# Three more attention units by rows, their projections spread, and the loads of the next group moved to other slots

## The chip, the cores and the metric

The kernel runs on one core of one Trainium2 chip. The metric is the device time of one launch in microseconds (us), the median of several runs. A profile is one of those executions; its "span" is some 2 us shorter than the device time. A run is called fast when it lies within 1.5% of the fastest run of the same kernel; only fast runs are compared.

## The reference, cut to what matters

One block with adaptive layer norms: grouped-query attention over a cache, then a gated MLP with a spatial projection.

```python
h = _layernorm(x, axis=-1) * (1 + ca) + sa          # sa, ca, ga, sb, cb, gb = split(silu(c) @ w_mod)
q = (h @ wq) ...                                     # 2048 rows, 32 heads of 128
scores = einsum('bhqd,bhkd->bhqk', q, k) * Dh ** -0.5  # 8 groups of K and V, 4 heads each, 2048 keys
o = einsum('bhqk,bhkd->bhqd', softmax(scores), v)
x = x + ga * (o @ wo)
... # second norm and the MLP, gated by gb
```

## The kernel before

The work is cut into 128 **units**: 8 groups of 4 heads times 16 tiles of 128 query rows. A unit has 8 **slots**; a slot is two QK matmuls of 512 columns (they make the scores) and one exponential on 128x1024. PV is the product of these exponentials with V. A unit is done in one of two ways. By columns, the scores come out transposed, PV needs 64 matmuls of 129 columns, and a small transpose by DMA (oT) follows. By rows, the scores come out with queries on partitions, each head is normalised on VectorE and turned by a DMA transpose of 128x2048 (pT; a **turn** below), and PV needs 16 matmuls of 512 columns, two units later than by columns. Even units from `TURN_A` on go by rows. The normalised and not yet turned rows of a head sit in `pn`, four buffers, each used again two units later.

```python
TURN_A, TURN_B = 3 * CT, (HKV - 1) * NT              # 12 and 112; CT = 4, NT = 16

def by_rows(u):
    return TURN_A <= u < TURN_B and u % 2 == 0

def pv_at(u):
    return u + 3 if by_rows(u) else u + 1            # so unit TURN_A + 1 has no PV: the "hole"

def turn_rows(u, hh):                                # two slots after a head's last exponential
    ...
    nc.vector.tensor_scalar(out=pn[hh], in0=pn[hh], scalar1=rinv, scalar2=None, op0=ALU.mult)
    nc.sync.dma_start_transpose(out=pTs[u][:, :, hh * P : (hh + 1) * P], in_=pn[hh])
```

`at(unit, slot, fn)` puts work at a place of the program. This is an order of issue per engine and no time: GpSimd, which has little to do, reaches a load long before TensorE reaches the slot, unless something stops it.

```python
ln1_at(1, (0, 7), (1, 2), (2, 2))     # chunk 1 of 4: statistics, norm (+ 4 DMA transposes), modulation
ln1_at(2, (2, 4), (3, 1), (4, 5))
ln1_at(3, (5, 1), (5, 5), (7, 4))
at(2, 5, lambda: nc.gpsimd.dma_start(out=wmod_b, in_=wmod_dram[:, :, 2 * D : NMOD]))   # 2 MB
at(9, 4, mod_cols_b)
at(10, 4, mod_rows)

def mod_rows():                       # the two gate rows, ga and gb
    ...                               # 32 matmuls of one column, result on partitions
    for i, (part, rows) in enumerate(((2, ga_rows), (5, gb_rows))):
        ...
        line = dram.tile([D], FP32, name=f"mod{part}")
        nc.gpsimd.dma_start(out=line[:].rearrange("(dt p) -> p dt", p=P), in_=modc[:, cols])
        nc.gpsimd.dma_start(out=rows[:], in_=line[:].partition_broadcast(P))
```

The last two lines, twice, are **the chain of the gate rows**: 2 KB written to memory as 512 pieces of 4 bytes, and read back to all partitions (256 KB).

Of the kernel before, what the change touches and what calls it, by code (L numbers as in the profile page):

```python
# [575 lines left out]
def kernel(  # L576
# [19 lines left out]
    nc = tc.nc  # L596
    _, S, D = A_x.shape
    _, HKV, SK, DH = A_k_cache.shape
# [4 lines left out]
    NMOD = w_mod.shape[1]  # L603
    assert DH == P and D == 512 and S % 512 == 0 and SK % 1024 == 0 and FH % P == 0 and REP == 4
    NT = S // P
# [4 lines left out]
    CT = 512 // P  # L610
    FC = _f_chunk(FH)
    NFHC = FH // FC
    NSLOT = NKT // 2
# [12 lines left out]
    wmod_dram = w_mod.rearrange("(p dt) n -> p dt n", p=P)  # L626
# [35 lines left out]
    wmod_b = wspp.tile([P, NDT * 4 * D], BF16, name="wsp")[:].rearrange(  # L662
        "p (k n) -> p k n", k=NDT
    )
# [53 lines left out]
    def load_wq(g, engine):  # L718
        wqs[g] = early.tile([P, NDT, REP * DH], BF16, name="wq_g")
        engine.dma_start(  # L720
            out=wqs[g][:], in_=wq_dram[:, :, g * REP * DH : (g + 1) * REP * DH]
        )

    def load_v(g):
        v1 = late.tile([P, NKT, DV], BF16, name="v1")
        nc.gpsimd.memset(v1[:, :, DH:DV], 1.0)
        if g > 0:
            nc.gpsimd.dma_start(out=v1[:, :, 0:DH], in_=v_dram[:, g])
        else:
            nc.sync.dma_start(out=v1[:, 0 : NKT // 2, 0:DH], in_=v_rows)  # L730
            nc.sync.dma_start(
                out=v1[:, NKT // 2 : NKT, 0:DH], in_=v_dram[:, 0, NKT // 2 : NKT]
            )
        groups[g]["v1"] = v1

    def load_wo(g, engine):
        wo_g = late.tile([P, REP, D], BF16, name="wo_g")
        engine.dma_start(out=wo_g[:], in_=wo_dram[:, g * REP : (g + 1) * REP, :])
        groups[g]["wo"] = wo_g

    def load_k(g):
        kT = early.tile([P, SK], BF16, name="kT")
        nc.sync.dma_start_transpose(out=kT[:], in_=A_k_cache[0, g])
        groups[g] = dict(kT=kT)
# [154 lines left out]
    for k in range(2):  # L899
        for dt in (2 * k, 2 * k + 1):  # L900
# [3 lines left out]
            else:  # L904
                nc.scalar.activation(
                    out=dst,
                    in_=src,
# [17 lines left out]
    for hf, copy in enumerate((nc.vector.tensor_copy, nc.scalar.copy)):  # L925
        copy(
            out=qTs[0][:, 2 * hf : 2 * hf + 2, 0:P],
            in_=q_ps[hf][:, 0 : 2 * P].rearrange("p (h q) -> p h q", h=2),
# [3 lines left out]
    def qproj(b, heads, c0, n, banks=("misc", "misc")):  # L932

        g, ch = divmod(b, NCH)
        if b not in qTs:
            qTs[b] = early.tile([P, REP, 512], BF16, name="qT")
        one = n * len(heads) <= 512
        ps = {}

        def mm(hh, dt):  # L940
            if dt == 0 and (not one or hh == heads[0]):
                ps[0] = bank(banks[hh % 2])
            o0 = (hh - heads[0]) * n if one else 0
            nc.tensor.matmul(  # L944
                ps[0][:, o0 : o0 + n],
                lhsT=wqs[g][:, dt, hh * DH : (hh + 1) * DH],
                rhs=hTs[ch][:, dt, c0 : c0 + n],
                start=(dt == 0),
                stop=(dt == NDT - 1),
            )  # L950
            if dt == NDT - 1 and (not one or hh == heads[-1]):
                hs = heads if one else [hh]
                dst = qTs[b][:, hs[0] : hs[-1] + 1, c0 : c0 + n]
                src = ps[0][:, 0 : len(hs) * n].rearrange("p (h q) -> p h q", q=n)
                nc.vector.tensor_copy(out=dst, in_=src)  # L955

        return [lambda hh=hh, dt=dt: mm(hh, dt) for hh in heads for dt in range(NDT)]
# [4 lines left out]
    NU = HKV * NT  # L962


    TURN_A, TURN_B = 3 * CT, (HKV - 1) * NT

    def by_rows(u):
        return TURN_A <= u < TURN_B and u % 2 == 0
# [7 lines left out]
    def at(it, slot, fn):  # L976
        later.setdefault((it, slot), []).append(fn)
# [230 lines left out]
    def ln1_at(ch, stats, norm, turn):  # L1208
        st = {}
        at(*stats, lambda: st.update(r=ln1_stats(ch * CT, CT)))  # L1210
        at(*norm, lambda: st.update(x=ln1_norm(ch * CT, CT, st["r"])))
        at(norm[0], norm[1] + 1, lambda: ln1_dma(ch * CT, CT, st["x"]))
        at(*turn, lambda: ln1_dma_mod(ch))
# [1 line left out]
    ln1_at(1, (0, 7), (1, 2), (2, 2))  # L1215
    ln1_at(2, (2, 4), (3, 1), (4, 5))
    ln1_at(3, (5, 1), (5, 5), (7, 4))
    at(2, 5, lambda: nc.gpsimd.dma_start(out=wmod_b, in_=wmod_dram[:, :, 2 * D : NMOD]))
    at(TURN_B + 3, 5, lambda: nc.gpsimd.dma_start(out=win_sb, in_=win_dram))
    at(9, 4, mod_cols_b)  # L1220
    at(10, 4, mod_rows)

    def set_fill(b):


        hole = TURN_A + 1 if (TURN_A + 1) // CT == b - 1 else None
        fs = qproj(b, list(range(REP)), 0, 512, ("misc", "o_ps" if hole else "misc"))
        for k, fn in enumerate(fs):
            it, slot = (b - 1) * CT + k // NDT, k % NDT
            if hole:  # L1230
                it, slot = hole, k // 2
            if b == 1:
                it, slot = 2 + (10 + k) // 16, (5 + k // 2) % 8
            elif b == 2:
                it, slot = (5, k // 2) if k < 8 else (it, slot)
            fill.setdefault((it, slot), []).append(fn)

    def wsp0():
# [4 lines left out]
        at(TURN_B + 4 + st // 2, 2 + 4 * (st % 2), lambda st=st: load_wsp(wsp[0], 0, st))  # L1243
    for g in range(1, HKV):
        it = (g - 1) * NT
        at(it + 7, 6, lambda g=g: load_k(g))
        at(it + 8, 3, lambda g=g: load_v(g))
        at(it + 9, 3, lambda g=g: load_wo(g, nc.gpsimd))
        at(it + 7, 3, lambda g=g: load_wq(g, nc.gpsimd))


    zs = {}
# [90 lines left out]
    for it in range(NU + 6):  # L1343
        if it < NU:
            if it % CT == 0 and it // CT + 1 < NB:
                set_fill(it // CT + 1)
        elif it == NU:
            free_a.close()
            z2p = fast.enter_context(tc.tile_pool(name="z2p", bufs=1))
            zs["z2"] = z2p.tile([P, NT, FH], BF16, name="z2")  # L1350
# [41 lines left out]
    for f in range(NFT):  # L1392
# [6 lines left out]
        out=ok1[:], in0=rall[:], scalar1=1.0 / SAFE, scalar2=None, op0=ALU.is_ge  # L1399
# [8 lines left out]
        out=bad[:], in0=okm[:], scalar1=-1.0, scalar2=1.0, op0=ALU.mult, op1=ALU.add  # L1408
# [137 lines left out]
```

## Time and profile before

| | before |
|---|---|
| device time, median of 4 runs | 1317.82 us (1315.36 to 1318.52) |
| span of the profiled run | 1314.1 us, granted clock 0.999 (share of TensorE's full clock) |
| pair of units by rows and by columns, steady state | 17.44 us |
| units 0 to 15, from the first exponential of 0 to that of 16 | 138.5 us |

The duration of a unit is read from the timeline of ScalarE: it is the distance between the first exponentials of two units. All unit durations below come from this view. The first fence is GpSimd's timeline (start, duration, instruction, idle time before it and what ended it), the second the timeline of the queue that issues the transposes.

```profile
113.98 0.56 POOL L1174 DMA_DIRECT2D ga_rows<-mod  x1 [8.27 <-DMA mod<-modc]
114.53 0.76 POOL L1173 DMA_DIRECT2D mod<-modc  x1
126.35 0.55 POOL L1174 DMA_DIRECT2D gb_rows<-mod  x1 [11.05 <-DMA mod<-modc]
```

```profile
121.41 12.66 SPq L1038 DMA_TRANSPOSE pT<-win_sb  x3
```

The chain runs from 104.96 us (the first write) to 126.35. The first turn of all is issued at 121.41, so the writes and the turns share only the last 5 us.

### The profile page before, as it was taken

The page shows a single profiled execution, that of the slowest core. Times are in us where ns is not written, and L with a number is a line of the kernel's source. Part 1 is how long each engine was busy: PE and PEld are TensorE (multiplying, and loading weights), DVE is VectorE, ACT ScalarE, POOL GpSimd, SP SyncE. Part 2 cuts the span into 40 slices and gives each one's busy share as a digit, 9 for nine tenths or more (in the row PEclk, how much of TensorE's full clock was granted, in tenths as well). Part 3 has the DMA queues.
Part 4 walks back from the last instruction along what each step waited for, and adds up shares of the span by engine and source line. Part 5 has one row for each costly group of instructions (what it writes and reads, how often), then busy time and mean ns, then how long its engine had stood idle before and what let it go on. Part 6 is the DMA issues. An engine that isn't in the chain of part 4 may idle for free.

```text
span 1314.1 us, 25092 instructions
## 1 busy us (share of the span) xinstructions
PE 1305.1 (99%) x9959; PEld 755.5 (57%) x9959; DVE 657.4 (50%) x1612; ACT 1105.0 (84%) x1461; POOL 52.0 (4%) x96
## 2 busy tenths in 40 slices
PE   9999999999999999999999999999999999999998
PEld 5666555555555555555555555555556666644445
DVE  6624445444454544444455544444452566784444
ACT  7899999999999999999999999999998899650000
POOL 1101000000000000000000000000000000120000
PEclk9999999999999999999999999999999999999999
DMA  7554988878988888988897877688762232143200
GB/s 181 123 67 58 180 161 141 140 125 158 153 144 138 144 141 138 135 142 157 153 143 129 155 141 144 124 166 151 140 126 76 45 62 48 29 117 80 69 21 27
DMA packets 537741, 156.79 MB, mean 119 GB/s; under 512 B 527280, under 2 KB 533680, under 8 KB 537616
## 3 DMA queue, kind: packets, MB, share of 16 engines
q1 hardware_dynamic: 530592, 135.97, 60.3%
q0 software_dynamic: 4432, 16.91, 4.6%
q10 hardware_dynamic: 2592, 2.23, 0.5%
q8 instruction: 80, 1.31, 0.4%
q14 instruction: 45, 0.37, 0.1%
HBM read 21.89 MB, written 2.10 MB: 18 GB/s over the span
## 4 chain that ended last, share of the span: by engine, by line
PE 98%; DMA 1%; DVE 0%; issue 0%; ACT 0%; ACTq 0%; DVEq 0%
PE o_ps L1069 21%; PE s_ps L1013 20%; PE o_ps L1048 13%; PE s_ps L994 13%; PE misc L1101 8%; PE misc L944 8%; PE misc L1426 7%; PE s_ps L1260 2%; PE s_ps L1299 2%; PE o_ps L1447 1%; DMA pT<-wmod_a 1%; PE o_ps L785 1%; PE s_ps L1447 1%; PE misc L854 0%; PE o_ps L944 0%; DVE hT L813 0%
## 5 line engine op out<-in xcount | busy, mean ns | idle before, releaser
L1020 ACT ACTIVATE wsp<-s_ps 128x1024 bf16<-128x1024 f32 x408 | 416.2, 1025 | 19.5 <-PE s_ps L1013 3.5
L1013 PE MATMUL s_ps<-qT,kT 128*128 128x512 bf16 x1248 | 370.9, 379 | 1.9 <-ACT wmod_a L1001 1.6
L1001 ACT ACTIVATE win_sb<-s_ps 128x1024 bf16<-128x1024 f32 x300 | 307.0, 1025 | 6.2 <-ACT win_sb L1001 0.8
L1069 PEld LDWEIGHTS <-wsp 128*128 128x128 bf16 x3264 | 218.5, 98 | 96.3
L1069 PE MATMUL o_ps<-v,wsp 128*128 128x129 bf16 x3264 | 251.6, 220 | 0.0
L994 PE MATMUL s_ps<-kT,qT 128*128 128x512 bf16 x800 | 237.9, 379 | 0.0
L1048 PE MATMUL o_ps<-pT,v 128*128 128x512 bf16 x800 | 237.3, 379 | 0.0
L1020 ACT ACTIVATE pT<-s_ps 128x1024 bf16<-128x1024 f32 x216 | 217.3, 1026 | 20.6 <-PE s_ps L1013 8.3
L1101 PE MATMUL misc<-wo_g,oT 128*128 128x512 bf16 x512 | 194.0, 379 | 0.0
L1013 PEld LDWEIGHTS <-kT 128*128 128x128 bf16 x1248 | 121.0, 98 | 117.0 <-issue 4.4
L944 PE MATMUL misc<-hT,wq_g 128*128 128x512 bf16 (+2 forms) x520 | 187.0, 371 | 0.1
L1069 PEld LDWEIGHTS <-pT 128*128 128x128 bf16 x1728 | 115.3, 98 | 49.6
L955 DVE CAST qT<-misc 128x512 bf16<-128x512 f32 x125 | 85.5, 684 | 112.2 <-PE misc L944 112.2
L1048 PEld LDWEIGHTS <-v 128*128 128x128 bf16 x800 | 78.2, 98 | 94.4
L1069 PE MATMUL o_ps<-v,pT 128*128 128x129 bf16 x1728 | 132.5, 220 | 0.0
L1057 DVE CAST oT<-o_ps 128x512 bf16<-128x512 f32 x50 | 34.6, 691 | 173.7 <-PE o_ps L1048 173.7
L1035 DVE TENSOR_SCALAR win_sb<-win_sb,rall 128x2048 bf16<-128x2048 bf16 x150 | 113.0, 753 | 5.7 <-DVE rall L1034 0.5
L994 PEld LDWEIGHTS <-qT 128*128 128x128 bf16 x800 | 78.2, 98 | 52.5 <-issue 0.2
L1001 ACT ACTIVATE wmod_a<-s_ps 128x1024 bf16<-128x1024 f32 x100 | 102.4, 1024 | 2.3 <-DMA pT<-wmod_a 2.3
L1426 PE MATMUL misc<-wsp,z 128*128 128x512 bf16 (+2 forms) x560 | 100.7, 336 | 0.0
L1080 DVE RECIPROCAL rall<-o_ps 128x2 f32<-128x2 f32 x156 | 26.6, 170 | 135.1 <-PE o_ps L1069 131.4
L1031 DVE TENSOR_TENSOR tot<-rs 128x1 f32<-128x1 f32 x200 | 30.7, 154 | 120.6 <-ACT win_sb L1001 119.1
(106 smaller groups left out, 856.5 us busy)
## 6 DMA issues: line engine op xcount, KB each, us to landing
wq_g<-in_A_wq_dram POOLq DMA_DIRECT2D x7, 512.0 KB, 5.5
v<-in_A_v_cache_dram POOLq DMA_DIRECT2D x7, 512.0 KB, 5.9
wo_g<-in_A_wo_dram POOLq DMA_DIRECT2D x7, 512.0 KB, 3.8
pT<-win_sb SPq DMA_TRANSPOSE x150, 4.9
wsp<-in_w_mod_dram POOLq DMA_DIRECT2D x1, 2048.0 KB, 10.4
out_dram<-yout ACTq DMA_DIRECT2D x16, 128.0 KB, 1.7
win_sb<-in_B_w_in_dram POOLq DMA_DIRECT2D x1, 1792.0 KB, 9.3
x_sb<-in_A_x_dram SPq DMA_DIRECT2D x3, 512.0 KB, 5.3
```

The source lines that it names most:

```text
L944: nc.tensor.matmul(ps[0][:, o0 : o0 + n], lhsT=wqs[g][:, dt, hh * DH : (hh + 1) * DH], rhs=hTs[ch][:, dt, c0 : c0 + n], start=(dt == 0), s ...
L955: nc.vector.tensor_copy(out=dst, in_=src)
L994: nc.tensor.matmul(s_ps[:, c * 512 : (c + 1) * 512], lhsT=qTs[b][:, hh, jj * P : (jj + 1) * P], rhs=groups[g]["kT"][:, k0 : k0 + 512], sta ...
L1001: nc.scalar.activation(out=pn[hh][:, half * HK : (half + 1) * HK], in_=s_ps[:], func=ACT.Exp, scale=inv_sqrt_dh, accum_out=rsums[u][:, i : ...
L1013: nc.tensor.matmul(s_ps[:, h * 512 : (h + 1) * 512].rearrange("p (r q) -> p r q", r=REP), lhsT=groups[g]["kT"][:, kt * P : (kt + 1) * P], ...
L1020: nc.scalar.activation(out=pTs[u][:, 2 * i : 2 * i + 2, :], in_=s_ps[:].rearrange("p (k q) -> p k q", k=2), func=ACT.Exp, scale=inv_sqrt_dh,)
L1035: nc.vector.tensor_scalar(out=pn[hh], in0=pn[hh], scalar1=rinv, scalar2=None, op0=ALU.mult)
L1048: nc.tensor.matmul(o_pss[u][:], lhsT=groups[g]["v1"][:, kt, 0:DH], rhs=pTs[u][:, kt, :], start=(kt == 0), stop=(kt == NKT - 1),)
L1057: nc.vector.tensor_copy(out=oTs[u][:], in_=o_pss[u][:].rearrange("p (r q) -> p r q", r=REP))
L1069: nc.tensor.matmul(o_ps[:, hh % 2, 0 : DH + 1], lhsT=pTs[u][:, kt, hh * P : (hh + 1) * P], rhs=groups[g]["v1"][:, kt, 0 : DH + 1], start=( ...
L1101: nc.tensor.matmul(X_ps[:], lhsT=oTs[u][:, hh, :], rhs=groups[g]["wo"][:, hh, :], start=(hh == 0), stop=(hh == REP - 1),)
L1426: nc.tensor.matmul(g_ps[:, :n], lhsT=z2[:, st, f * P : (f + 1) * P], rhs=wsp[t][:, st, c0 : c0 + n], start=(st == 0), stop=(st == NT - 1 a ...
```

## The change

Its intent: more units by rows, since those cost TensorE less; the projections that fill the unit without PV spread a little around it; and one load of the next group per pair of units, at a slot where the pair's turns are done. An earlier first unit by rows forces the w_mod work forward: `wmod_b` sits in the buffer that unit `TURN_A + 1` writes.

```diff
-    TURN_A, TURN_B = 3 * CT, (HKV - 1) * NT
+    TURN_A, TURN_B = CT + 2, (HKV - 1) * NT
...
-    at(2, 5, lambda: nc.gpsimd.dma_start(out=wmod_b, in_=wmod_dram[:, :, 2 * D : NMOD]))
+    at(2, 1, lambda: nc.gpsimd.dma_start(out=wmod_b, in_=wmod_dram[:, :, 2 * D : NMOD]))
...
-    at(9, 4, mod_cols_b)
-    at(10, 4, mod_rows)
+    at(4, 4, mod_cols_b)
+    at(5, 4, mod_rows)
... # in set_fill
             if hole:
-                it, slot = hole, k // 2
+                it, slot = divmod(hole * NSLOT + k // 2 - 1, NSLOT)
             if b == 1:
                 it, slot = 2 + (10 + k) // 16, (5 + k // 2) % 8
-            elif b == 2:
-                it, slot = (5, k // 2) if k < 8 else (it, slot)
... # for each next group g, it = (g - 1) * NT
-        at(it + 7, 6, lambda g=g: load_k(g))
-        at(it + 8, 3, lambda g=g: load_v(g))
-        at(it + 9, 3, lambda g=g: load_wo(g, nc.gpsimd))
-        at(it + 7, 3, lambda g=g: load_wq(g, nc.gpsimd))
+        at(it + 7, 4, lambda g=g: load_wq(g, nc.gpsimd))
+        at(it + 9, 5, lambda g=g: load_k(g))
+        at(it + 11, 4, lambda g=g: load_v(g))
+        at(it + 13, 4, lambda g=g: load_wo(g, nc.gpsimd))
```

## The prediction

> **What bounds the kernel now.** I read the page first, then the chain of work that ended last, then the timeline of ScalarE (one exponential per slot, so it clocks the loop), then windows of single pairs of units, and last the GpSimd timeline and the landing times of DMAs, because the change moves issues of DMAs.
>
> ```profile
> PE 1305.1 (99%) x9959; PEld 755.5 (57%) x9959; DVE 657.4 (50%) x1612; ACT 1105.0 (84%) x1461; POOL 52.0 (4%) x96
> ...
> PE 98%; DMA 1%; DVE 0%; issue 0%; ACT 0%; ACTq 0%; DVEq 0%
> ```
>
> TensorE is busy for 1305.1 of 1314.1 us and makes 98% of the chain: the kernel is a stream of matmuls. Busy alone would not prove that, since matmuls overlap, so I checked the pace. This is ScalarE's timeline, at the first exponentials of units 34, 35 and 36 (start, duration, instruction), and then the window over that pair and over one unit of the last group, where all units are by columns (length, then busy us of PE, PEld, DVE, ACT, POOL with counts, clock, DMA share, GB/s).
>
> ```profile
> 306.72 1.02 ACT L1001 ACTIVATE win_sb<-s_ps 128x1024 bf16<-128x1024 f32 x1
> ...
> 315.54 8.52 ACT L1020 ACTIVATE wsp<-s_ps 128x1024 bf16<-128x1024 f32 x8
> ...
> 324.16 1.02 ACT L1001 ACTIVATE win_sb<-s_ps 128x1024 bf16<-128x1024 f32 x1
> ```
>
> ```profile
> 306.72:324.16 17.44, 17.44 (x132) 9.87 (x130) 8.48 (x22) 17.00 (x24) 1.24 (x2) 1.00 0.88 159
> ...
> 1028.50:1037.30 8.80, 8.80 (x92) 5.97 (x90) 4.96 (x12) 8.19 (x8) 0.82 (x2) 1.00 0.29 61
> ```
>
> The even unit takes 8.82 us, the odd one 8.62, a pair 17.44, and a unit of pure columns 8.80. In the odd unit TensorE does 40 matmuls of 512 columns (16 QK, 16 PV by rows, 4 output projection, 4 query projection): 8.62 / 40 = 215.5 ns each. The even one has 24 of them (5.17) and the 64 PV matmuls of 129 columns of the odd unit before it: (8.82 - 5.17) / 64 = 57.0 ns. With these two numbers the pure unit comes to 24 x 0.2155 + 64 x 0.057 = 8.82, as seen. So the pace is matmul issue, at full clock. The other fact in those windows: a pair by rows has DMA busy 0.88 (four transposes of 128x2048), a unit by columns 0.29.
>
> **What the Trainium skill says.** "TensorE: Matmul & The Clock Gate", section "Wait — 56ns, not 53.3ns?", gives warm start-to-start times of 55.6 ns at 128 columns and 215.7 ns at 512; the trace agrees (57.0 at 129, 215.5 at 512). "Perfetto Trace Analysis", section "Sequencer Loop", says that an engine instruction waits for its semaphores and resources, and so not for the place in the program at which other engines are; the trace agrees, below. "DMA: Bandwidth & Descriptors", section "Issuing engines are not separate DMA queues", says that DMAs of all issuers run on the same 16 engines and interleave, and its section "Queues, rings and completion order" that each engine goes round robin between queues by whole packets; the trace agrees in direction, as transposes land late beside a GpSimd load.
>
> **The change, part by part.**
>
> 1. Three more units by rows (6, 8, 10; 53 instead of 50). PV by columns costs 64 x 57.0 ns = 3.65 us, by rows 16 x 215.5 ns = 3.45. All of it lies on TensorE, the bound: 3 x 0.20 = **0.6 us gained**. The weights, QK and projections are the same; each unit adds four normalisations on VectorE (0.75 us each by the row of L1035) and four transposes on the DMA queue, and drops one small transpose and four small VectorE operations. VectorE, at 8.48 of 17.44 us, has room.
>
> 2. The unit without PV moves from 13 to 7. Before, units 12 to 15 start at 118.03, 126.23, 134.13 and 142.52, and unit 16 at 149.76: 31.73 us. TensorE's work in them is 7.96 (no query projection), 7.76 (16 of them, no PV), 7.96 and 6.90 us = 30.58. So 1.15 us is lost where ScalarE or a transpose is the limit. After, query projections of block 2 start one slot early and fill unit 7 as (16 + 15 + 4) x 0.2155 = 7.54 us; unit 6 has 8.18, unit 8 8.82, unit 9 7.76 us. These stand closer to what ScalarE can follow (7.24 by columns, about 8.2 by rows, from those units), so I take 0.3 us lost in place of 1.15: **0.8 us gained**.
>
> 3. Loads "one per pair of units when the turns are done". Here is the GpSimd queue before, whole lines of its timeline.
>
> ```profile
> 21.77 1.05 POOL L681 TENSOR_TENSOR rstd_ln<-ve_ln,mhalf 128x4 f32<-128x4 f32 x1
> ...
> 36.09 1.04 POOL L681 TENSOR_TENSOR rstd_ln<-ve_ln,mhalf 128x4 f32<-128x4 f32 x1
> 37.09 0.95 POOL L1218 DMA_DIRECT2D wsp<-in_w_mod_dram  x1
> ...
> 59.11 0.82 POOL L720 DMA_DIRECT2D wq_g<-in_A_wq_dram  x1
> ...
> 60.11 1.31 POOL L728 DMA_DIRECT2D v<-in_A_v_cache_dram  x1
> 61.41 0.76 POOL L738 DMA_DIRECT2D wo_g<-in_A_wo_dram  x1
> 104.96 0.76 POOL L1173 DMA_DIRECT2D mod<-modc  x1 [42.79 <-DVE modc L1171]
> ```
>
> The program has wq, v and wo of group 1 in units 7, 8 and 9 (from 72 us on), but all three are issued within 2.3 us at 59 us, in unit 5. GpSimd runs ahead until a buffer or an operand stops it. For later groups the waits say what stops it: the last query projection of two groups ago (64.7 us for wq), the last PV (55.5 for v), an output projection (16.2 for wo). The change keeps the order wq, v, wo, and frees no buffer earlier, so for groups 2 to 7 these 18 loads stay where they are. Only the K load, on the queue of the transposes, really moves, by about two units, from just behind a fourth turn to just behind a fourth turn. **Gain: none.** The 2.1 us that ScalarE waits at 540 us for a late transpose, issued at 528.82 together with a wq load, can come back.
>
> 4. The load of the second part of w_mod moves from unit 2, slot 5 to unit 2, slot 1. By the program that is half a unit. On GpSimd it is much more: the operation before it was the rstd of chunk 2 (ends 37.13, load issued 37.09); now it is that of chunk 1 (ends 22.82). So this 2 MB load goes out near 22.8 us, at the moment of the four transposes of the normalised rows of chunk 1 (issued 23.3 to 27.3). What a GpSimd load does to such transposes is on the trace: their landing times (min, median, max) in chunk 1 with no load beside them, chunk 2 beside the w_mod load, and chunk 3 beside wq, v and wo.
>
> ```profile
> DMA to landing us min/median/max: 2.5/3.5/4.5
> ```
>
> ```profile
> DMA to landing us min/median/max: 6.0/6.9/7.8
> ```
>
> ```profile
> DMA to landing us min/median/max: 8.5/11.4/13.7
> ```
>
> In chunk 2 the load took 10.4 us (37.09 to 47.5) and the last transpose landed at about 49.1 (43.1 + 6.0), 1.6 us behind it. In chunk 1 of the changed kernel that gives 22.8 + 10.4 + 1.6 = 34.8 us in place of 30.4. And chunk 1 is the urgent one. On the timeline of before:
>
> ```profile
> 30.57 1.38 DVE L813 TENSOR_SCALAR hT<-hT,modc 128x512 bf16<-128x512 bf16 x4 [3.02 <-DMA hT<-xn]
> ...
> 32.12 0.59 PE L944 MATMUL misc<-hT,wq_g 128*128 128x512 bf16 x2
> ```
>
> VectorE already waits 3.0 us here, and the query projection starts 1.5 us after VectorE does. A landing at 34.8 puts the first projection at about 35.3: TensorE stops for 3.2 us, in order, with nothing to put in front. VectorE's backlog behind it (four statistics, 3.3 us, ahead of the first copy of a projection) may cost another 0.5. **3.7 us lost**, on the path.
>
> 5. w_mod's other matmuls and the gate rows move from units 9 and 10 to 4 and 5. Same work (two times 0.8 us on TensorE). But the chain of their GpSimd DMAs (104.96 to 126.35 before, 21 us, two waits of 8.3 and 11.1) now stands ahead of wq, v and wo of group 1: they go out at about 84 us, all three together, in unit 8, where four turns of 128x2048 are issued (at +3.4, +5.8, +9.0, +12.5 us as in unit 58). Beside such a burst chunk 3's transposes landed up to 13.7 us late. A turned buffer is written again after 12 to 14 us, so a stall of 0 to 4 us for ScalarE, and TensorE after it: **1.3 us lost**, a guess in the middle.
>
> Sum: -0.6 - 0.8 + 3.7 + 1.3 = +3.6 us: 1317.1 + 3.6 = 1320.7. I shade this to **1320.0 us**, since the two losses are less sure than the gains.
>
> **Rivals.**
> (a) The early load does no harm: the first transposes pass before its data starts, the rest share the engines. For it: 1.5 us of slack, and the DMA share in 27 to 36 us is only 0.34. Against it: both collisions on the trace held transposes to the end of the load. Then 1316 to 1317.
> (b) The spread does what it means to: the late transpose at 540 us and any like it vanish, worth 2.1 us in the profiled run. Against it: issues are set by buffers, not by slots. With (a) it gives 1314 to 1315.
> (c) Turns become the bound in units 6 to 12. For it: DMA share is 0.88 in each pair, and 0.99 in 118 to 150 us, where the gate rows, wq and turns met, so a backlog drains slowly. Against it: that meeting cost only 0.2 us of ScalarE's wait. It would add 3 to 6 us: 1323 to 1326.
>
> **Range and chances.** The three runs of before spread over 3.2 us. Losses of 0 to 9 us against gains of 1.4 to 3.5 give 1314 to 1325; I take 1314.5 to 1324.5. Two per cent is 26 us, more than any term here can make: faster 0.01, same 0.97, slower 0.02.
>
> **What would show it.** 192 fewer PV matmuls of 129 columns and 48 more of 512. The w_mod load issued near 23 us, not 37; VectorE waiting about 7 us for the transposes of chunk 1; the first query projection of block 1 near 35 us; unit 4 starting at 49 to 50 us instead of 45.98. wq, v and wo of group 1 issued within 3 us of each other near 84. Units 12 on at 17.44 us a pair, loads of groups 2 to 7 at the same phase as before. I am wrong if unit 4 starts within 1 us of 46 (step 4), if GpSimd's loads appear at their program slots (step 3), or if pairs after unit 12 take other than 17.44 us.

## The result, and the profile after

The changed kernel takes **1330.61 us** (median of 4 runs, 1328.79 to 1331.96) against 1317.82. The ratio is 1.010, with a 95% interval of 1.008 to 1.0119. Here and below a ratio is the mean time of one kernel's fast runs over that of the other's of the same rounds, so it is not quite the ratio of the medians. The loss is some 13 us; the prediction had 1320.0 and a range that ended at 1324.5.

These are the lines of the page after that answer to the first two of the prediction: the busy time by engine, and the chain that ended last.

```profile
PE 1309.4 (99%) x9815; PEld 751.7 (57%) x9815; DVE 669.9 (50%) x1639; ACT 1107.7 (83%) x1485; POOL 51.8 (4%) x96
...
PE 97%; DMA 2%; DVE 0%; ACT 0%; issue 0%; SPq 0%; DVEq 0%; ACTq 0%
```

TensorE has 144 matmuls less, as it should (192 of 129 columns gone, 48 of 512 added), and is still busy 99%. DMA took one per cent of the chain from it. A page over a span of 1300 us can hardly show more than that, so the units have to be laid side by side.

| unit | before | after | what it has after |
|---|---|---|---|
| 2 | 8.46 | **13.11** | first projections of chunk 1 |
| 3 to 5 | 27.77 | 27.58 | |
| 6 | 8.81 | 8.95 | first unit by rows |
| 7 | 8.81 | 7.69 | the hole |
| 8 | 8.81 | **19.13** | |
| 9 | 9.61 | 9.42 | |
| 10 to 15 | 50.10 | 52.27 | |
| 0 to 15 | 138.53 | 154.33 | |
| pair from unit 16 on | 17.44 | 17.44 | |

From unit 16 on the two kernels run at the same pace. The loss is in two units. In unit 2, first on VectorE and TensorE, then on ScalarE:

```profile
34.59 1.38 DVE L813 TENSOR_SCALAR hT<-hT,modc 128x512 bf16<-128x512 bf16 x4 [6.99 <-DMA hT<-xn]
35.05 0.70 PE L944 MATMUL misc<-hT,wq_g 128*128 128x512 bf16 x2 [2.72 <-DVE hT L813]
...
36.27 1.02 ACT L1020 ACTIVATE pT<-s_ps 128x1024 bf16<-128x1024 f32 x1 [3.21 <-PE s_ps L1013]
```

VectorE waits 7.0 us for the transposes of chunk 1 where it waited 3.0 before, and the projection starts at 35.05 in place of 32.12. In unit 8, TensorE's and ScalarE's waits:

```profile
93.51 0.39 PE L1101 MATMUL misc<-wo_g,oT 128*128 128x512 bf16 x1 [4.17 <-DMA oT<-onorm]
...
94.61 1.02 ACT L1001 ACTIVATE win_sb<-s_ps 128x1024 bf16<-128x1024 f32 x1 [4.53 <-PE s_ps L994]
```

```profile
101.91 1.02 ACT L1001 ACTIVATE wmod_a<-s_ps 128x1024 bf16<-128x1024 f32 x1 [6.18 <-DMA pT<-wmod_a]
```

Two transposes are late one after the other: the small oT of unit 5, and the fourth turn of unit 6, whose `pn` buffer unit 8 wants to write. This is GpSimd's queue after:

```profile
22.82 0.96 POOL L1218 DMA_DIRECT2D wsp<-in_w_mod_dram  x1
...
64.56 0.83 POOL L1173 DMA_DIRECT2D mod<-modc  x1
74.01 0.58 POOL L1174 DMA_DIRECT2D ga_rows<-mod  x1 [8.62 <-DMA mod<-modc]
74.58 0.76 POOL L1173 DMA_DIRECT2D mod<-modc  x1
85.63 0.55 POOL L1174 DMA_DIRECT2D gb_rows<-mod  x1 [10.29 <-DMA mod<-modc]
86.17 0.76 POOL L720 DMA_DIRECT2D wq_g<-in_A_wq_dram  x1
...
87.06 1.18 POOL L728 DMA_DIRECT2D v<-in_A_v_cache_dram  x1
88.21 0.85 POOL L738 DMA_DIRECT2D wo_g<-in_A_wo_dram  x1
```

The w_mod load is at 22.8 us, as predicted. wq, v and wo go out within 2.1 us, at 86 us, as predicted (84). And the chain of the gate rows now runs from 64.6 to 85.6 us, over the turns of unit 6. The queue of the transposes shows what that did:

```profile
71.60 14.04 SPq L1038 DMA_TRANSPOSE pT<-win_sb  x3
85.75 1.22 SPq L1089 DMA_TRANSPOSE oT<-onorm  x1
87.07 7.65 SPq L1038 DMA_TRANSPOSE pT<-wmod_a  x1
```

The queue issues in order and one at a time. Three turns kept it for 14.0 us, so oT, whose input VectorE had ready before 77 us, was issued at 85.75 only. The fourth turn was issued at 87.07, inside the burst of loads, kept the queue 7.65 us and landed 14.7 us after its issue.

So there were three suspects for unit 8: the burst of loads, the chain of the gate rows, or units by rows so early in themselves.

### The profile page after: what moved, and what is told of

The parts are those of the page before. It is cut to its first block, busy times and chain, and to the rows that moved or that the text cites. A ratio compares the mean times of both kernels' runs of the same rounds, so it can differ in the third digit from the quotient of the medians.

```text
span 1328.1 us, 24918 instructions
## 1 busy us (share of the span) xinstructions
PE 1309.4 (99%) x9815; PEld 751.7 (57%) x9815; DVE 669.9 (50%) x1639; ACT 1107.7 (83%) x1485; POOL 51.8 (4%) x96
## 4 chain that ended last, share of the span: by engine, by line
PE 97%; DMA 2%; DVE 0%; ACT 0%; issue 0%; SPq 0%; DVEq 0%; ACTq 0%
PE o_ps L1069 20%; PE s_ps L1013 19%; PE o_ps L1048 14%; PE s_ps L994 14%; PE misc L1101 8%; PE misc L944 8%; PE misc L1424 7%; PE s_ps L1258 2%; PE s_ps L1297 2%; PE o_ps L1445 1%; DMA pT<-wmod_a 1%; PE s_ps L1445 1%; DMA hT<-xn 0%; DMA wmod_a<-in_w_mod_dram 0%; PE misc L854 0%
## 5 line engine op out<-in xcount | busy, mean ns | idle before, releaser
L1020 ACT ACTIVATE wsp<-s_ps 128x1024 bf16<-128x1024 f32 x432 | 441.3, 1024 | 22.4 <-PE s_ps L1013 5.3
L1001 ACT ACTIVATE win_sb<-s_ps 128x1024 bf16<-128x1024 f32 x318 | 325.4, 1024 | 11.4 <-PE s_ps L994 5.0
L1069 PEld LDWEIGHTS <-wsp 128*128 128x128 bf16 x3456 | 232.2, 98 | 102.4 <-issue 0.8
L1069 PE MATMUL o_ps<-v,wsp 128*128 128x129 bf16 x3456 | 267.3, 220 | 0.0
L994 PE MATMUL s_ps<-kT,qT 128*128 128x512 bf16 x848 | 252.8, 380 | 0.2 <-ACT win_sb L1001 0.2
L1048 PE MATMUL o_ps<-pT,v 128*128 128x512 bf16 x848 | 252.3, 380 | 0.0
L1020 ACT ACTIVATE pT<-s_ps 128x1024 bf16<-128x1024 f32 x168 | 168.0, 1027 | 19.9 <-PE s_ps L1013 11.1
L1069 PEld LDWEIGHTS <-pT 128*128 128x128 bf16 x1344 | 90.4, 98 | 38.6 <-issue 0.6
L1069 PE MATMUL o_ps<-v,pT 128*128 128x129 bf16 x1344 | 103.8, 221 | 0.0
L1424 PEld LDWEIGHTS <-z 128*128 128x128 bf16 x560 | 50.6, 98 | 48.5
```

The costliest lines, as they stand in the source:

```text
L994: nc.tensor.matmul(s_ps[:, c * 512 : (c + 1) * 512], lhsT=qTs[b][:, hh, jj * P : (jj + 1) * P], rhs=groups[g]["kT"][:, k0 : k0 + 512], sta ...
L1001: nc.scalar.activation(out=pn[hh][:, half * HK : (half + 1) * HK], in_=s_ps[:], func=ACT.Exp, scale=inv_sqrt_dh, accum_out=rsums[u][:, i : ...
L1020: nc.scalar.activation(out=pTs[u][:, 2 * i : 2 * i + 2, :], in_=s_ps[:].rearrange("p (k q) -> p k q", k=2), func=ACT.Exp, scale=inv_sqrt_dh,)
L1048: nc.tensor.matmul(o_pss[u][:], lhsT=groups[g]["v1"][:, kt, 0:DH], rhs=pTs[u][:, kt, :], start=(kt == 0), stop=(kt == NKT - 1),)
L1069: nc.tensor.matmul(o_ps[:, hh % 2, 0 : DH + 1], lhsT=pTs[u][:, kt, hh * P : (hh + 1) * P], rhs=groups[g]["v1"][:, kt, 0 : DH + 1], start=( ...
L1424: nc.tensor.matmul(g_ps[:, :n], lhsT=z2[:, st, f * P : (f + 1) * P], rhs=wsp[t][:, st, c0 : c0 + n], start=(st == 0), stop=(st == NT - 1 a ...
```

## The experiments

Unit durations of all runs, in us (each kernel's own profile), and times. Kernels with the same letter ran on the same chip and share its runs of before. The kernel before ran 1319.39 us on A, 1316.78 on B and 1315.03 on C.

| run | unit 2 | 6 | 7 | 8 | 9 | 22 | time, us | ratio to before (95%) |
|---|---|---|---|---|---|---|---|---|
| after | 13.11 | 8.95 | 7.69 | 19.13 | 9.42 | 8.82 | 1330.61 | 1.010 (1.008 to 1.0119) |
| e1_wmod_back (A) | 8.46 | 9.01 | 7.69 | 20.59 | 7.73 | 8.82 | 1328.67 | 1.0078 (1.0048 to 1.0108) |
| e2_gated (A) | 12.62 | 8.89 | 7.69 | 14.32 | 7.89 | 8.82 | 1323.34 | 1.0032 (1.0001 to 1.0064) |
| e3_burst_no_modline (A) | 13.14 | 8.64 | 7.70 | 8.59 | 7.89 | 19.17 | 1327.43 | 1.0079 (1.0039 to 1.0119) |
| e5_gated_no_modline (A) | 11.51 | 8.64 | 7.70 | 8.59 | 7.89 | 19.74 | 1328.32 | 1.0078 (1.0047 to 1.0109) |
| e6_writes20_spread36 (B) | 11.57 | 8.64 | 7.69 | 8.59 | 7.89 | 10.10 | 1317.31, one run | none |
| e7_pe_rows (B) | 8.46 | 8.64 | 7.69 | 8.59 | 7.89 | 8.82 | 1315.42 | 0.9986 (0.9968 to 1.0005) |
| e8_line_at_end (B) | 8.46 | 8.64 | 7.69 | 8.59 | 7.89 | 8.82 | 1313.60 | 0.9983 (0.9959 to 1.0008) |
| e11_half_wmod_early (C) | 9.90 | 8.64 | 7.69 | 8.59 | 7.89 | 8.82 | 1318.45 | 1.0021 (1.0003 to 1.004) |
| e12_writes_together (C) | 8.47 | 8.97 | 7.69 | 18.68 | 7.89 | 8.82 | 1323.36 | 1.0061 (1.0037 to 1.0084) |
| e10_before_line_end (B) | 8.46 | 8.81 | 8.81 | 8.81 | 9.61 | 8.82 | 1314.92 | 0.9982 (0.9963 to 1.0001) |
| e4_before_wmod_early (C) | 12.91 | 8.81 | 8.81 | 8.81 | 9.61 | 8.82 | 1321.45 | 1.004 (1.002 to 1.006) |
| e9_before_line20 (C) | 8.46 | 8.81 | 8.81 | 8.81 | 9.61 | 17.09 | 1324.97 | 1.0067 (1.0045 to 1.0089) |

All twelve gave correct results, and all runs compared by time are in the fast state; e6 ran once, so its state is unknown and its unit durations alone are used. The times of one kernel vary by several us (those of before from 1313.9 to 1323.4 on chip B). Each column of durations comes from one execution, and that one need not be typical: the profiled run took 1324.75 us in e1, 1327.91 in e4 and 1314.28 in e11, against medians of 1328.67, 1321.45 and 1318.45.

**e1_wmod_back**: the w_mod load back at its old slot.

```diff
-    at(2, 1, lambda: nc.gpsimd.dma_start(out=wmod_b, in_=wmod_dram[:, :, 2 * D : NMOD]))
+    at(2, 5, lambda: nc.gpsimd.dma_start(out=wmod_b, in_=wmod_dram[:, :, 2 * D : NMOD]))
```

> The changed kernel with one thing undone: the 2 MB load of w_mod is again at unit 2, slot 5. My theory (the early load holds back the four transposes of chunk 1, and VectorE, then TensorE, wait for them): the load is issued near 37 us, those transposes land by 31 us as before, unit 2 takes 8.5 us in place of 13.1, unit 8 stays slow (17 to 20 us), and the time falls by 4.6 us to about 1326. Rival, that the units by rows make the whole loss: unit 2 stays at 13 us, time 1330 to 1331.

Unit 2 fell from 13.11 to 8.46 us: four slots of program order on GpSimd were worth 4.65 us. Unit 8 stayed slow (20.59). The time fell by less than expected: the median is 1328.67 (the profiled run took 1324.75), against 1330.61 of the changed kernel, which was measured in other rounds.

**e2_gated**: the loads held to their slots. A one-column memset by VectorE in the tile makes GpSimd's load wait for VectorE to get there.

```diff
+    def gate(ap):
+        nc.vector.memset(ap, 0.0)
...
     def load_wq(g, engine):
         wqs[g] = early.tile([P, NDT, REP * DH], BF16, name="wq_g")
+        gate(wqs[g][:, 0, 0:1])
... # the same in load_v and load_wo, for g > 0
```

> The changed kernel in which each load of wq, v and wo of the next group waits for a small memset of VectorE in the tile it fills, at the load's own slot, so that GpSimd can't run ahead: one load per pair of units, as the change meant it. If the burst of three loads at 86 to 88 us makes the 10.3 us lost in unit 8: unit 8 takes 8.8 to 9.5 us and the time is about 1320.5. If the chain of small DMAs for the gate rows (64 to 86 us), which runs beside the first turns, makes it: unit 8 still takes 15 us or more, time 1327 to 1330. If both have to meet: 1 to 3 us left, 1321 to 1323. If units by rows so early are the cause by themselves: nothing changes, 1330.

Unit 8 fell to 14.32 us, between the outcomes that I had written for one cause or the other, and well above what I had written for both having to meet. So the burst has a share. But the gates moved only v and wo (to 120.28 and 137.72 us). wq stood behind the chain in GpSimd's queue until its own slot had passed, and went out right after it, 1.3 us ahead of the fourth turn:

```profile
86.87 1.18 POOL L724 DMA_DIRECT2D wq_g<-in_A_wq_dram  x1
```

The 5.7 us that stay (14.32 less the 8.59 of e3 and e5) are therefore the chain with one load, and not the chain alone.

**e3_burst_no_modline**: the burst kept at unit 8, the chain of the gate rows moved to unit 20.

```diff
-            nc.vector.tensor_copy(out=modc[:, cols], in_=mc_ps[:, i * NDT : (i + 1) * NDT])
+            tmp = modt[:, i * NDT : (i + 1) * NDT]
+            nc.vector.tensor_copy(out=tmp, in_=mc_ps[:, i * NDT : (i + 1) * NDT])
+            at(*MODLINE, lambda ...: mod_line(part, rows, cols, tmp))   # MODLINE = (20, 4); copy to modc, write, broadcast
... # cut: wq of group 1 gated at unit 8, slot 1; v and wo ungated behind it
```

> The changed kernel in which the DMAs of the gate rows (two writes of 2 KB by elements and two broadcasts) wait until unit 20, and the burst of wq, v and wo stays in unit 8 (wq waits for VectorE at unit 8, slot 1; v and wo follow at once). If the burst alone makes the loss, unit 8 still takes 15 us or more, or unit 10 does, and the time is 1327 to 1330. If the chain of the gate rows alone does, unit 8 takes under 9.5 us, time about 1320.5. If both have to meet: unit 8 to 10 lose 1 to 3 us, 1321 to 1323.

This run settles most of it. With the burst at 84.6 us and no chain, unit 8 takes 8.59 us: the burst alone, at this place, cost nothing. And unit 22, two units after the place to which the chain went, takes 19.17 us in place of 8.82. The loss moved with the chain. The queue of the transposes in this run, to be held against the fence of the changed kernel above:

```profile
71.40 7.99 SPq L1042 DMA_TRANSPOSE pT<-win_sb  x3
79.49 1.21 SPq L1093 DMA_TRANSPOSE oT<-onorm  x1
80.80 1.93 SPq L1042 DMA_TRANSPOSE pT<-wmod_a  x1
```

The same three turns, issued at the same time, keep the queue for 8.0 us in place of 14.0; oT goes out 6.3 us earlier, and the fourth turn keeps the queue 1.9 us in place of 7.65.

**e5_gated_no_modline**: both, loads held to their slots and the chain at unit 20.

> Both at once: loads of the next group held to their slots, and the gate rows' DMAs in unit 20. By any theory in which loads and turns collide, units 6 to 11 take what TensorE needs, 8.2, 7.7, 8.8, 7.8, 8.8 and 8.6 us, and only unit 2's 4.6 us are left: 1317.8 + 4.6 - 1.4 = 1321. If units by rows so early are the cause by themselves, unit 8 stays at 19 us and the time at 1330.

Units 6 to 11 took 8.64, 7.70, 8.59, 7.89, 8.77 and 8.62 us, what TensorE and ScalarE need: units by rows so early do no harm. But my expected time was wrong by 7 us, because I had thought of the chain as harmless at unit 20, without a burst beside it: unit 22 took 19.74 us. In steady flow the chain alone costs 10.9 us.

**e6_writes20_spread36**: which half of the chain. The two element writes at unit 20, one behind the other; the two broadcasts gated at unit 36.

> Which half of the gate rows' chain stalls the turns. As e5_gated_no_modline, but only the two writes of 2 KB by elements (512 pieces of 4 bytes each) go at unit 20; the two broadcasts of 256 KB wait for VectorE until unit 36. If the element writes hold the turns back: unit 22 takes 17 to 20 us as in e5, unit 38 under 9.5. If the broadcasts do: unit 22 takes 8.8 and unit 38 12 us or more. Unit 2 keeps its 3 to 4.6 us.

At the writes, turns landed 12.7 and 15.0 us after their issue; at the broadcasts one took 8.9 and the rest 4.3 to 5.1. Unit 38 showed nothing. So the broadcasts by themselves cost nothing. But unit 22 took 10.10 us, neither 8.8 nor the 17 to 20 that I had expected: the writes by themselves cost 1.3 us of the 10.9 of the full chain. With no broadcast between them both writes had landed within 16 us (191.7 to 207.4), where the writes of e5 took 24 (191.9 to 215.5). A turned buffer is written again after 12 to 14 us (the figure is the prediction's), so it fits that the longer the writes last, the more turns come too late; it is not shown, since the broadcast between the writes is gone too.

**e12_writes_together**: the other use of that, e1 with both writes first and then both broadcasts.

> Another dose: e1 (the changed kernel with w_mod's load back) in which GpSimd issues both element writes one behind the other and the two broadcasts after them, so that the writes overlap (16 us in all, as e6 showed) rather than follow each other (21 us), and the burst of wq, v and wo, ungated, goes out about 10 us earlier. If the time of writes beside turns sets the loss, unit 8 takes 9 to 14 us in place of the 20.6 of e1. If the burst sets it, 15 or more.

A miss: unit 8 took 18.68 us. The writes were over at about 69 us, but GpSimd was then free, broadcasts and all three loads went out between 68.6 and 72.6 us, beside the turns of unit 6, and the loads took 11 to 16 us each; a turn issued at 70.09 landed at 89.67. In e3 the same burst had found the turns of unit 6 done, and only the first turn of unit 8 was issued (at 87.62) while the loads were in flight; it landed after 9.3 us, and no unit lost by it. So a burst of loads does cost, when it falls on several turns, and this run leaves open what e6 had left open. The share of v and wo in the changed kernel is the difference between after and e2, 6.4 us over units 6 to 9 (45.19 - 38.79).

**e9_before_line20**: the kernel before with the chain moved to unit 20 and nothing else.

> The kernel before with only the gate rows' DMA chain moved to unit 20, where turns are in steady flow and no load of the next group goes out. By my theory (element writes beside turns hold the transposes up) unit 22 takes 15 to 20 us in place of 8.8, and the time is 6 to 11 us over before, about what the whole change lost. If the harm needs the early units by rows or the burst, unit 22 stays under 9.5 and the time is that of before.

Unit 22 took 17.09 us and the time rose by 10 us. This is ScalarE's timeline of that run where its waits were longest:

```profile
211.98 1.02 ACT L1001 ACTIVATE win_sb<-s_ps 128x1024 bf16<-128x1024 f32 x1 [5.82 <-DMA pT<-win_sb]
...
232.38 1.02 ACT L1001 ACTIVATE win_sb<-s_ps 128x1024 bf16<-128x1024 f32 x1 [2.70 <-DMA pT<-win_sb]
```

The second wait, in unit 24 (12.85 us), I had not expected: wq, v and wo of group 2 stood behind the chain in GpSimd's queue and went out together at 212.6 to 214.6 us, again a burst on turns: a turn issued at 212.76 landed at 232.28, just after wo (232.08). A change of place of four DMAs makes three quarters of the loss of the whole change, without a single unit by rows more.

**e10_before_line_end**: the kernel before with the chain behind the last turn, at unit 111.

> The kernel before with the gate rows' DMAs moved to unit 111 and nothing else. In the kernel before this chain lay almost wholly ahead of the first turn, so I expect 0 to 0.6 us gained (units 12 to 15 take 31.2 to 31.7 in place of 31.7). Against it e8 shows what units by rows from 6 on are worth when no DMA meets another: by my count of matmuls 1.4 us for e8.

Units 12 to 15 took 31.62 us in place of 31.73: where it stood before, the chain cost 0.1 us, so no wait of an engine could warn of it. The queue of the transposes could. This line is to be held against the one of before (121.41, 12.66 us for the same three turns):

```profile
121.14 7.92 SPq L1038 DMA_TRANSPOSE pT<-win_sb  x3
```

Five shared microseconds had already kept this queue 4.7 us longer. The slack of the turned buffers hid it.

**e4_before_wmod_early** and **e11_half_wmod_early**: the early w_mod load alone, and half of it.

> The kernel before with one part of the change: w_mod's second load from unit 2, slot 5 to slot 1. If that alone makes the stall in unit 2: the load goes out at 22.8 us, unit 2 takes 11.5 to 13.1 us in place of 8.46, all else as before, and the time is 3 to 4.7 us over before. If the stall needs another part of the change, unit 2 stays at 8.5. Beside it: if the late transpose at unit 60 belongs to the kernel before and is no accident, units 60 and 61 again take about 1 to 2 us too long.

Unit 2 took 12.91 us, so no other part of the change is needed for that stall. (In this profile units 14 and 92 too were held by late turns; at 92 a turn and a wq load issued within 0.1 us of each other took 14.3 and 12.1 us. The like happened at unit 60 in before and in e10. It comes and goes between runs, and none of my runs says why.)

> A dose: e8 with half of w_mod's load (1 MB) at unit 2, slot 1 and the other half at slot 5. If the transposes of chunk 1 wait for the end of the load beside them, they land near 22.8 + 5.5 + 1.6 = 30 us as without it, VectorE waits 3 us as before, and unit 2 takes 8.5 us, so the time is that of e8. If any load at that place harms as much, unit 2 takes 11 to 13 us.

The dose works, though I had put its threshold too high: the half load took 6.5 us, the last transpose of chunk 1 landed at 32.94 us, between the 30.44 of before and the 34.46 of after, and unit 2 took 9.90, between 8.46 and 13.11.

**e7_pe_rows** and **e8_line_at_end**: the version without the meetings. In both, w_mod's load is at its old slot and the loads are gated. e7 has no chain at all, TensorE makes the gate rows already broadcast; e8 keeps the chain, at unit 111.

```diff
+    # e7, cut: sc_bc[kt] is made by VectorE just before
+    for row, rows in ((0, ga_rows), (3, gb_rows)):
+        mr_ps = bank("misc")
+        for kt in range(NDT):
+            nc.tensor.matmul(mr_ps[:], lhsT=sc_bc[kt][:],       # silu(c) broadcast to 128 columns
+                             rhs=wmod_b[:, kt, row * D : (row + 1) * D],
+                             start=(kt == 0), stop=(kt == NDT - 1))
+        nc.vector.tensor_copy(out=rows[:], in_=mr_ps[:])
```

> The changed kernel without all the meetings: w_mod's load back at unit 2, slot 5, loads of wq, v and wo held to their slots, and no DMA at all for the gate rows: TensorE makes them already broadcast, with eight matmuls of 512 columns (1.7 us) in place of 32 of one column (0.8). If the DMA meetings are the whole loss, no unit from 2 on takes over 9.7 us but unit 3 and the doubled one at 113, and the span is that of e5 less 3.0 (unit 2) less 10.9 (unit 22) plus 0.9: about 1312.5 against 1314.1 of before, 0.1 to 0.3 per cent faster. If units by rows this early cost something by themselves, it is slower than before.

> As e7, but with the gate rows' DMAs kept and moved behind the last turn, to unit 111. If the writes harm only turns beside them, no unit is slow, and the time is about 1 us under that of e7. If they also hold the four-column or small transposes of the last group, units 112 to 116 lose 1 to 5 us.

e8 has no slow unit, and units 0 to 15 take 137.3 us against 138.5 of before: the gain that the change was made for exists, and is 1.2 us. Its median is 1313.60 us against 1316.78, its interval (0.9959 to 1.0008) just includes no difference, and one of its six runs took 1320.68. e7 loses 2.5 us in unit 5 (11.22 in place of 8.71; I had expected 0.9) and is at 1315.42, with six runs within 0.6 us. Most of the surprise is a wait of TensorE of 1.65 us there for VectorE, which makes the broadcast silu(c) only behind four layer norm statistics. Both medians lie some 15 us and more under that of the changed kernel, and 1.4 and 3.2 us under that of before. But e10, which has no more units by rows than before, is at 1314.92: against it the gain of e8 is 1.3 us, and e7 has none.

## Why the prediction was wrong, point by point

**What bounds the kernel, and the pace: right.** Pairs of the steady state that no late turn holds up take 17.44 us in all runs.

**Steps 1 and 2, units by rows and the hole: right.** Predicted 1.4 us gained; e8 shows 1.2 over units 0 to 15 against before, and 1.1 against e10.

**Step 3, the loads do not follow their slots: right.** Three loads went out in 2.1 us, at 86 where I had 84, and wq of later groups at the phase of before (in unit 27: 4.1 us behind its start in both). "Perfetto Trace Analysis", section "Sequencer Loop", which says that an instruction waits for its own semaphores, is borne out by e2: v and wo, made to wait for a memset of VectorE, went out at 120.28 and 137.72 us in place of 87.06 and 88.21.

**Step 4, the early w_mod load: right in mechanism, 3.7 us predicted, 4.65 measured.** The transposes landed at 34.46 (predicted 34.8), the projection started at 35.05 (35.3). What I left out is the clock. Here are two windows of the changed kernel, one over the wait and one over the rest of unit 2, and then the same two of e5 (length, busy us of PE, PEld, DVE, ACT and POOL, granted clock, DMA share, GB/s).

```profile
32.00:36.00 4.00, 1.28 (x10) 0.63 (x8) 1.41 (x5) 1.06 (x2) 0.00 (x0) 1.00 0.72 119
36.00:40.57 4.57, 4.57 (x30) 2.96 (x29) 4.36 (x13) 2.05 (x2) 0.68 (x2) 0.63 0.00 2
```

```profile
32.00:36.00 4.00, 1.23 (x12) 0.68 (x10) 1.26 (x4) 1.17 (x2) 0.00 (x0) 1.00 0.79 129
36.00:39.06 3.06, 3.06 (x31) 2.00 (x30) 2.92 (x10) 2.05 (x2) 0.00 (x0) 1.00 0.00 0
```

After nearly the same wait of TensorE (2.72 and 2.77 us) the clock dropped to a mean of 0.63 in one run and not in the other: about 4.57 x 0.37 = 1.7 us more, and unit 2 took 13.11 and 11.51. "TensorE: Matmul & The Clock Gate", section "What's actually happening", has the array at half clock after an idle window of about 3.4 us; in these runs a gap of 2.7 us was enough, but not each time. In unit 8 the mean clock was 0.72 from 92 to 98 us.

**Step 5, the step that failed.** The prediction put it as "a stall of 0 to 4 us for ScalarE, and TensorE after it: **1.3 us lost**, a guess in the middle", from wq, v and wo in one burst beside the turns. What it measured: units 6 to 9 took 45.19 us in the changed kernel and 32.81 in e8, so 12.4 us. Two things were wrong in it. First the cause: I saw the chain of the gate rows only as a delay for the loads behind it, and took the loads for the harm. e3 (burst, no chain: nothing lost), e5 and e9 (chain, no burst beside it: 10.9 and 8.3 us in unit 22) show that the chain itself holds the turns up. In the changed kernel 6.0 us come from the chain with wq behind it (units 6 to 9 take 38.79 us in e2), and 6.4 from v and wo, which fall on turns already late; the time lost to a dropped clock is within both. Without the chain the burst costs nothing at this place, so the two parts are not independent.

Second the evidence: against rival (c), turns as the bound, I wrote "that meeting cost only 0.2 us of ScalarE's wait". 16 of the chain's 21 us lay ahead of the first turn. A number from a place where two things overlap by a quarter was used for a place where they overlap wholly, and it was a wait, which slack had hidden, where the queue of the transposes showed the harm (12.66 us against the 7.92 of e10). Also, chunk 3's transposes had not landed "up to 13.7 us late" but 13.7 us after their issue, where the median with no load beside them was 3.5. Rival (c) came nearest, but not for its reason: turns by themselves are no bound (e5 and e8 take 8.6 us in unit 8), and its 1323 to 1326 was still too low by 5 us.

How 2 KB can do this is settled only in part. From 64.5 to 74 us one of the writes, five small transposes and the first turn are under way in the changed kernel; e3, without the write, has the same transposes at the same times to 0.3 us, and its second turn from 73.48 on. DMA engines were busy for 0.90 of that time and moved 63 GB/s with the write, and 0.51 and 100 GB/s without it. The first line is of after, the second of e3.

```profile
64.50:74.00 9.50, 9.50 (x98) 6.50 (x97) 5.38 (x15) 8.70 (x15) 0.89 (x2) 1.00 0.90 63
```

```profile
64.50:74.00 9.50, 9.50 (x101) 6.61 (x100) 5.21 (x15) 9.20 (x17) 0.00 (x0) 1.00 0.51 100
```

The write's own packets do not fill that time. By the DMA view of the same window of after (packets, MB, share of the 16 engines' time), the queue of the write, q0, has 2.1% of it, and that of the transposes, q1, has 87.7%:

```profile
q1 hardware_dynamic: 2464, 0.60, 87.7%
q0 software_dynamic: 32, 0.00, 2.1%
```

What the traces do show is an order of landing. In all fourteen profiles together, 40 transposes were issued while one of these writes was in flight (counting those for which both landings are recorded), and none landed before the write had; 26 that had been issued earlier landed while a write was in flight. With every DMA of GpSimd counted, the loads too, it is 310 transposes, and again none landed first. So a transpose issued beside a transfer of GpSimd did not land before that transfer, whatever its bytes: the 2 MB of w_mod beside chunk 1 took 9.95 us to land, the second write of 2 KB 10.77. Both losses of the change fit this one order.

Why 2 KB stay in flight so long: "DMA: Bandwidth & Descriptors", section "Specifications", says that below 512 B a transfer is not at line rate and is done as read-modify-write, and the program asks here for 512 elements of 4 B, each at its own place in memory. It fits, but no run wrote the same 2 KB in one piece, so that the small pieces are the reason is not shown.

**The sum.** +4.65 (unit 2) + 12.4 (units 6 to 9) - 1.2 (the intended gain) = 15.8 us, which is the difference of units 0 to 15 (154.33 - 138.53). The profile of before also had an accident of 1.8 us at units 60 and 61 that this run had not, which leaves 14.0, the difference of the spans.

## What to carry to other kernels

An instruction's place in the program of an engine that runs ahead is no time: before moving an issue, look which instruction stands before it on its own queue, and what will be in flight at the moment that releases it. A stall read from a profile prices an overlap only as long as it was there, so measure how long two transfers were in flight together before carrying the price to another place, and look at the queue that was held as well as at the waits of the engines. And count a DMA by the time that it is in flight, not by its bytes: a chain of two writes of 2 KB and their broadcasts, beside turns of 2 MB a pair of units, cost more (10.9 us in e5) than everything that the change could gain.

## What the Trainium skill lacked or had wrong

- "DMA: Bandwidth & Descriptors", sections "Specifications" and "Queues, rings and completion order": small pieces are called slow for their own transfer. The second section says that a DMA's completion mark lands only after every earlier write of the same DMA engine, across its queues, and the landings here agree (40 of 40); it does not say how long small pieces can hold other queues up by this. Here a write of 2 KB in 512 pieces took 8.5 to 14.6 us, turns issued beside such writes landed 5.6 to 20.4 us after issue in place of mostly 4.3 to 6.2 (e8), and 9.5 us of window moved 63 GB/s in place of 100.
- The same page, section "Issuing engines are not separate DMA queues", calls the time of issue usually small relative to the DMA itself. Here the issue of one 128x2048 transpose kept its queue for 1.9 of the 4.3 us to its landing in e3, and for 7.65 of 14.7 in the changed kernel, and with it the turns behind it.
- "TensorE: Matmul & The Clock Gate", section "What's actually happening": half clock after an idle window of about 3.4 us. Here gaps of 2.72 and 2.77 us gave a mean clock of 0.63 in the next 4.6 us in one run, and 1.00 in the next 3.1 us in another.
